# A cosformer attention and token-mixing kernel: at most six DMA transfers in flight instead of eight

## The chip, the cores and the metric

The kernel runs on one core of a Trainium2 chip. The metric is device time in microseconds (us), the median of a few runs. The engines are named as in the profile: PE is TensorE's matmul, PEld its weight load, DVE is VectorE, ACT is ScalarE, POOL is GpSimd, SP is SyncE. SP computes nothing in this kernel; its queue issues all 138 DMA transfers.

## What is computed

The inputs q, k and v have the shape (8, 8, 576, 64): batch, heads, sequence, head width, in fp32. Linear attention with cosine and sine weights comes first, and a token mixer over its output second:

```python
theta = np.pi / 2.0 * pos / S
phi(x) = concatenate([relu(x) * cos(theta), relu(x) * sin(theta)], axis=-1)
kv  = einsum('bhsf,bhsd->bhfd', phi(k), v);  z = sum(phi(k), axis=2)
x   = einsum('bhsf,bhfd->bhsd', phi(q), kv) / (einsum('bhsf,bhf->bhs', phi(q), z) + 1e-06)
# heads joined: x is (8, 576, 512)
W   = (x @ w_q) @ (x @ w_k).T / sqrt(64)          # per batch, 576 x 576
out = relu(W @ x) @ w_out                         # (8, 576, 512), fp32
```

## The kernel before

**Tiling.** The eight heads of a batch are taken as four head pairs, and two head pairs make one work unit H, of which there are 16 (two for each batch). A unit needs 128 x 2 x 576 fp32 elements of each of q, k and v. These arrive as two halves, a and b, each a transfer of 128 x 576 fp32, 288 KB. For each input there are five raw buffers (NRAW, line 101), so unit H shares its buffer with units H-5 and H+5.

**Work of a unit.** RK and RQ (lines 222 to 227) take the ReLU of k and q into bf16. V reaches bf16, multiplied by the cosine and sine table, in one of two ways: by a cast CV (line 229) and a product VS on DVE (line 232), or by the one step VG on POOL (line 239, its instruction at line 248). PE then makes kv (KV, line 268), transposes q (QT, line 290) and multiplies the two (N, line 332, instructions at line 340). The evacuations and the division follow on DVE and ACT. When both units of a batch are there, the mixer runs: WK, WQ, KX, MX (lines 434 to 492), and for each pair of batches nine output tiles WO (line 504, matmuls at line 509), their copy OE to one of 18 output buffers (line 512), and their store ST of 256 KB (line 518).

**Weights.** LW (line 521) loads w_q and w_k (128 KB each) and w_out in four transfers of 256 KB.

**What sets the order.** The string ORDER (lines 26 to 67) is a list of words, each one step. The loop at line 555 calls them in this order, and every engine gets its instructions in the order of the calls. So the 138 transfers stand in SP's queue in the order of the words LQ, LK, LV, LW and ST. SP is strictly in order: an instruction that waits holds all transfers behind it. Nothing in the order is decided at run time; engines wait for each other by semaphores.

**What a transfer waits for before the change.** The framework gives the transfers eight semaphores in turn, named DMAHW0 to DMAHW7 in the listings. A transfer may be issued when the one that had its semaphore before it, eight transfers earlier, has landed; so no more than eight are ever in flight. Besides, a load waits until the readers of its raw buffer are through with it, and a store until its output buffer has been written.

Of the kernel before, what the change touches and what calls it, by code (L numbers as in the profile page):

```python
# [70 lines left out]
def kernel(  # L71
# [10 lines left out]
    nc = tc.nc  # L82
# [4 lines left out]
    P = 128  # L87
# [12 lines left out]

    NRAW, NPREP, NV2, NQM, NX, NXT, NOUT = (5, 2, 2, 2, 2, 2, 18)
    XC = DM // 2
    EPS_PE = (9, 17, 20, 21)
    NUM_JOINT = ()
    WARM_COLS = 384
# [8 lines left out]
    def bufs(n, shape, dtype, name):  # L114
        return [pool.tile(shape, dtype, name=f"{name}{i}") for i in range(n)]

    raw = {nm: bufs(NRAW, [P, 2, HC], FP32, f"{nm}raw") for nm in "kqv"}
# [10 lines left out]
    wq_b = bufs(2, [P, HS], BF16, "wq")  # L128
    kx_b = bufs(2, [P, 2, XC], BF16, "kx")
    mix_b = bufs(2, [P, NDM, 2 * S], BF16, "mix")  # L130
    o_b = bufs(NOUT, [P, DM], FP32, "o")

    PS = psum.tile([P, 8, 2048], U8, name="ps")
    place = {}

    def srcs(src):
        return [src[b].flatten().rearrange("(pr p e) -> p pr e", pr=NPAIR, p=P)
                for b in range(B)]

    src = {"k": srcs(k), "q": srcs(q), "v": srcs(v)}  # L140

    def load(nm, H, part):
        b, h = divmod(H, 2)
        for r in (0, 1) if part is None else (part,):
            nc.sync.dma_start(raw[nm][H % NRAW][:, r, :], src[nm][b][:, 2 * h + r, :])  # L145

    coef = math.pi / 2.0 / S
    ki = pool.tile([P, C, 2], I32, name="ki")
# [5 lines left out]
    wq_f = pool.tile([P, NDM, DH], FP32, name="wqf")  # L154
    wk_f = pool.tile([P, NDM, DH], FP32, name="wkf")
    wo_f = pool.tile([P, NDM, DM], FP32, name="wof")
# [50 lines left out]
    def cast(eng, dst, s):  # L207
        if eng is A:
            A.copy(dst, s)  # L209
        elif eng is G:  # L210
            G.tensor_scalar(dst, s, 1.0, 1.0, op0=ALU.mult, op1=ALU.mult)  # L211
        else:
            V.tensor_copy(dst, s)  # L213
# [111 lines left out]
    def num(t):  # L325
        return pair(t).bitcast(FP32)[:, :, 0:SC * (D + 1)].rearrange("p w (u e) -> p w u e", u=SC)
# [5 lines left out]
    def N(g, ps, eng):  # L332
# [3 lines left out]
        for u in range(SC):  # L336
            for s in range(2):
                for pr in range(2):
# [4 lines left out]
                        start=(u == 0 and s == 0),  # L343
                        stop=(u == SC - 1 and s == 1 and g not in EPS_PE))
        if g in EPS_PE:
            for pr in range(2):
# [4 lines left out]
    def rec(g):  # L351
        return rec_b[g // 2 % 4][:, g % 2]
# [24 lines left out]
    def RC(g, ps, eng):  # L377
        V.reciprocal(rec(g), num(place["N", g])[:, :, :, D:D + 1] if g in EPS_PE else rec(g))

# [51 lines left out]
    def bank(i):  # L431
        return PS[:, i, :].bitcast(FP32)
# [28 lines left out]
    def KX(b, ps, eng):  # L461
        place["KX", b] = ps
        o = bank(ps)
        for u in range(SC):
            for t in range(2):
                nc.tensor.matmul(  # L466
                    o[H2 * t:H2 * t + H2, 0:XC], wk_b[b % 2][:, u, :],
                    x_b[b % NX][:, u].rearrange("p h d -> p (h d)")[:, t * XC:(t + 1) * XC],
                    start=(u == 0), stop=(u == SC - 1))

    def XK(b, ps, eng):
        cast(eng, kx_b[b % 2][:, 0, :], bank(place["KX", b])[:, 0:XC])

# [42 lines left out]
    out_t = out.flatten().rearrange("(t p e) -> t p e", t=NT, p=P)  # L516

    def ST(i, ps, eng):
        nc.sync.dma_start(out_t[i], o_b[place["OE", i]])

    def LW(i, ps, eng):
        if i == 0:
            nc.sync.dma_start(wq_f, moe_w_q.rearrange("(c p) j -> p c j", p=P))
        elif i == 1:
            nc.sync.dma_start(wk_f, moe_w_k.rearrange("(c p) j -> p c j", p=P))
        else:
            nc.sync.dma_start(wo_f[:, i - 2, :], moe_w_out[(i - 2) * P:(i - 1) * P, :])

    def CW(i, ps, eng):
        if i < 2:  # L530
# [13 lines left out]
    def WU(i, ps, eng):  # L544
        n, shape = divmod(i, 4)
        rows, cols = ((H2, H2), (H2, P), (P, P), (P, H2))[shape]
        for _ in range(n):
            nc.tensor.matmul(bank(ps)[0:cols, 0:WARM_COLS], wc[0:rows, WARM_COLS:WARM_COLS + cols],
                             wc[0:rows, 0:WARM_COLS], start=True, stop=True)

    steps = {f.__name__: f for f in (EJ, XJ, RC, RJ, TB, WU, KV, QT, KE, QM, N, EP, X, XT, XR, XE, WK, KW, WQ, QW, KX, XK, XA, XB,
                                     MX, ME, WO, OE, ST, LW, CW, TK, TV, TI, TQ, TW, T2, TZ)}
    halves = {f.__name__: f for f in (RK, RQ, CV, VS, VG)}

    for word in ORDER.split():
        word, _, eng = word.partition("@")
        word, _, ps = word.partition(":")
        part = {"a": 0, "b": 1}.get(word[-1])
        word = word.rstrip("ab")
        kind = word[:2] if word[:2] in steps or word[:2] in halves or word[0] in "LT" else word[0]  # L560
        i, ps = int(word[len(kind):] or 0), int(ps or 0)
        if kind in ("LK", "LQ", "LV"):
            load(kind[1].lower(), i, part)
        elif kind in halves:
            halves[kind](i, ps, ENG.get(eng), slice(0, 2) if part is None else
                         slice(part, part + 1))
        else:
            steps[kind](i, ps, ENG.get(eng))
# [30 lines left out]
```

## Time and profile before

| what | value |
|---|---|
| median of 3 runs | 117.97 us (117.83 to 118.92) |
| the profiled execution: its own time | 116.73 us |
| the profiled execution: span of the instructions | 114.9 us |
| what lies around the span | 1.8 us |
| PE busy, share of the span | 96.4 us, 84% |
| DVE, ACT, POOL busy | 87.0, 84.2, 73.1 us |
| bytes by DMA, mean rate | 39.38 MB, 343 GB/s |
| granted TensorE clock | 1.000 |

The page names, for each group of instructions, the line of the kernel, the engine, out<-in by the program's tile names, how often it ran, its busy time and what its engine waited for. For a DMA, the SP row gives the time at which the transfer was issued and how long SP was held by issuing it; the data move later. "To landing" is the time from the start of the issue until the last byte is signalled. The chain that ended last is followed back from the last instruction, at each step to what released it.

### The profile page before, as it was taken

Reading aid. Unit: us, or ns where it says so; the run is one execution under the profiler, and the core shown is the slowest. Engines: PE = TensorE matmul, PEld = TensorE weight load, DVE = VectorE, ACT = ScalarE, POOL = GpSimd, SP = SyncE. Lnnn points to the kernel's source line nnn. Section 1 sums busy time; section 2 is a strip of 40 time slices with the busy share of each in tenths; the row PEclk is TensorE's granted clock in tenths of the full one; section 3 lists DMA queues with packets and bytes.
Section 4 is the critical chain, followed back from the end, with each engine's and each line's share of the span. In section 5 each row is a group of like instructions: output and inputs, shape, how many; then the busy total and the mean of one; then the engine's idle time right before and its main releaser. Section 6 shows DMA issues by size and latency. Waiting matters only on the chain.

```text
span 114.9 us, 4999 instructions
## 1 busy us (share of the span) xinstructions
PE 96.4 (84%) x2126; PEld 64.7 (56%) x2126; DVE 87.0 (76%) x160; ACT 84.2 (73%) x153; POOL 73.1 (64%) x62
## 2 busy tenths in 40 slices
PE   0034776797898999999899999999999999999970
PEld 0034644685776877656685656646774676563420
DVE  2029999699899999799579967699897896750650
ACT  7543518788999986999699959879788849568520
POOL 7434059965779799937899996799999821010000
PEclk9999999999999999999999999999999999999999
DMA  3999999999999999999999999989889679886494
GB/s 87 318 376 401 401 379 340 385 391 391 389 390 390 387 388 388 386 385 380 389 382 398 393 397 387 376 288 325 271 281 324 242 267 366 339 336 260 185 374 174
DMA packets 20662, 39.38 MB, mean 343 GB/s; under 512 B 3232, under 2 KB 3232, under 8 KB 20640
## 3 DMA queue, kind: packets, MB, share of 16 engines
q1 hardware_dynamic: 20640, 39.07, 93.4%
q8 instruction: 16, 0.26, 1.0%
q14 instruction: 6, 0.05, 0.1%
HBM read 29.62 MB, written 9.44 MB: 340 GB/s over the span
## 4 chain that ended last, share of the span: by engine, by line
PE 57%; DMA 32%; POOL 5%; SPq 2%; ACT 1%; issue 1%; POOLq 0%
PE ps L509 29%; DMA vraw<-in_v_dram 21%; DMA wkf<-in_moe_w_k_dram 6%; PE ps L340 5%; DMA qraw<-in_q_dram 5%; PE ps L285 5%; POOL v L248 4%; PE ps L489 4%; PE ps L466 3%; PE ps L419 3%; PE ps L439 3%; PE ps L452 3%; SPq L145 2%; PE ps L301 1%; PE ps L295 1%
## 5 line engine op out<-in xcount | busy, mean ns | idle before, releaser
L248 POOL TENSOR_TENSOR v<-vraw,vtab 128x1152 bf16<-128x1152 f32 (+1 forms) x16 | 49.4, 3098 | 9.3 <-DMA vraw<-in_v_dram 8.3
L509 PE MATMUL ps<-wow,mix 128*128 128x512 bf16 x144 | 34.9, 381 | 0.0
L393 DVE TENSOR_TENSOR x<-ps,rec 128x640 bf16<-128x640 f32 x32 | 25.3, 820 | 0.7
L509 PEld LDWEIGHTS <-mix 128*128 128x128 bf16 x144 | 12.4, 98 | 14.1 <-issue 1.6
L209 ACT COPY o<-ps 128x512 f32<-128x512 f32 x25 | 14.6, 587 | 5.9 <-PE ps L509 5.4
L500 ACT ACTIVATE mix<-ps 128x576 bf16<-128x576 f32 x27 | 16.9, 651 | 2.0 <-PE ps L489 1.8
L203 ACT ACTIVATE rk<-kraw 128x576 bf16<-128x576 f32 (+1 forms) x18 | 14.6, 817 | 2.2 <-DMA kraw<-in_k_dram 1.8
L316 DVE TENSOR_TENSOR qm<-ps,qtab 128x1152 bf16<-128x1152 bf16 x22 | 15.4, 747 | 0.3 <-PE ps L295 0.3
L340 PEld LDWEIGHTS <-qm 64*128 64x128 bf16 x640 | 12.5, 96 | 4.4 <-issue 3.0
L340 PE MATMUL ps<-kvs,qm 64*128 64x65 bf16 x640 | 14.2, 193 | 0.9 <-ACT kvs L209 0.8
L203 ACT ACTIVATE rq<-qraw 128x576 bf16<-128x576 f32 (+1 forms) x15 | 11.6, 784 | 4.5 <-DMA qraw<-in_q_dram 4.5
L295 PE MATMUL ps<-ident,rq 128*128 128x128 bf16 x99 | 8.2, 234 | 7.9 <-POOL rq L205 7.7
L285 PE MATMUL ps<-v,rk 64*64 64x130 bf16 x432 | 9.3, 227 | 3.5 <-DVE v L234 1.3
L213 DVE COPY o<-ps 128x512 f32<-128x512 f32 x11 | 7.6, 689 | 6.2 <-PE ps L489 3.7
L295 PEld LDWEIGHTS <-rq 128*128 128x128 bf16 x99 | 6.4, 105 | 9.5 <-POOL rq L205 7.9
L205 POOL TENSOR_SCALAR rq<-qraw 128x576 bf16<-128x576 f32 (+1 forms) x10 | 8.6, 868 | 4.3 <-DMA qraw<-in_q_dram 3.7
L285 PEld LDWEIGHTS <-rk 64*64 64x64 bf16 x432 | 7.4, 111 | 6.8 <-ACT rk L203 2.0
L209 ACT CAST kvs<-ps 128x260 bf16<-128x260 f32 (+1 forms) x14 | 6.2, 442 | 4.0 <-PE ps L285 3.3
L211 POOL TENSOR_SCALAR kx<-kx 64x256 bf16<-64x256 bf16 x5 | 2.0, 399 | 10.4 <-ACT kx L209 10.1
L209 ACT COPY xT<-ps 128x1280 bf16<-128x1280 bf16 (+1 forms) x7 | 8.2, 1176 | 0.1
L234 DVE TENSOR_TENSOR v<-vb,vtab 128x1152 bf16<-128x1152 bf16 (+1 forms) x9 | 8.2, 926 | 0.1
L213 DVE COPY xT<-ps 128x1280 bf16<-128x1280 bf16 (+1 forms) x9 | 7.2, 805 | 1.4 <-PE ps L406 0.8
(66 smaller groups left out, 131.9 us busy)
## 6 DMA issues: line engine op xcount, KB each, us to landing
qraw<-in_q_dram SPq DMA_DIRECT2D x32, 288.0 KB, 5.9
vraw<-in_v_dram SPq DMA_DIRECT2D x32, 288.0 KB, 5.9
kraw<-in_k_dram SPq DMA_DIRECT2D x32, 288.0 KB, 5.9
out_dram<-o SPq DMA_DIRECT2D x36, 256.0 KB, 3.7
wof<-in_moe_w_out_dram SPq DMA_DIRECT2D x4, 256.0 KB, 5.7
wqf<-in_moe_w_q_dram SPq DMA_DIRECT2D x1, 128.0 KB, 6.7
wkf<-in_moe_w_k_dram SPq DMA_DIRECT2D x1, 128.0 KB, 6.6
```

The lines of the kernel that those rows point to most:

```text
L203: A.activation(dst, s, AF.Relu)
L205: eng.tensor_scalar(dst, s, FMAX, 0.0, op0=ALU.min, op1=ALU.max)
L209: A.copy(dst, s)
L213: V.tensor_copy(dst, s)
L248: G.tensor_mul(dst[:, part, :, :, 0:D], s[:, part].unsqueeze(3).to_broadcast([P, n, C, 2, D]), vtab.unsqueeze(1).to_broadcast([P, n, C, 2, ...
L285: nc.tensor.matmul(kv_v[o, r, :], rk_of(H)[a, pr, c, :], v2_b[H % NV2][a, pr, c, :, 0:D + 1], start=(c == 0), stop=(c == C - 1))
L295: nc.tensor.transpose(qt_v[:, c, :], rq_b[H % NPREP][:, c, :, :], ident)
L316: V.tensor_mul(qm_b[H % NQM][:, :, r, 0:C, :], q_t[:, r].unsqueeze(1).to_broadcast([P, 2, C, H2]), qtab)
L340: nc.tensor.matmul(nv[:, pr, u, :], qm_b[H % NQM][a, s, r, 2 * u:2 * u + 2, :], kv_b[H % 2][a, r, pr if H in KV_WIDE else 0, s, 0:D + 1], ...
L393: V.tensor_tensor(x_b[b % NX][:, :, 4 * h:4 * h + 4, :].rearrange("p u (w r) d -> p r w u d", r=2)[:, r], nv[:, :, :, 0:D], rec(g).to_broa ...
L500: A.activation(dst, s, AF.Relu, scale=scale_moe)
L509: nc.tensor.matmul(o, mix_b[bp % 2][:, m, rt * P:(rt + 1) * P], wow[:, m, :], start=(m == 0), stop=(m == NDM - 1))
```

## The change

A helper `dma` issues every transfer and keeps a list of what it has issued. From the seventh transfer on, it adds a dependency on the transfer that was issued six earlier. The words, their order, the buffers and all other steps stay as they are.

```diff
+    IN_FLIGHT = 6
...
+    in_flight = []
+
+    def dma(dst, s):
+        i = nc.sync.dma_start(dst, s)
+        if len(in_flight) >= IN_FLIGHT:
+            tc.add_manual_dep(
+                i.ins, in_flight[-IN_FLIGHT].ins.name,
+                mybir.DependencyInfo(mybir.DependencyClass.Sync, mybir.DependencyReason.DATA),
+                reason="transfers in flight")
+        in_flight.append(i)
...
-            nc.sync.dma_start(raw[nm][H % NRAW][:, r, :], src[nm][b][:, 2 * h + r, :])
+            dma(raw[nm][H % NRAW][:, r, :], src[nm][b][:, 2 * h + r, :])
...
-        nc.sync.dma_start(out_t[i], o_b[place["OE", i]])
+        dma(out_t[i], o_b[place["OE", i]])
...
-            nc.sync.dma_start(wq_f, moe_w_q.rearrange("(c p) j -> p c j", p=P))
+            dma(wq_f, moe_w_q.rearrange("(c p) j -> p c j", p=P))
...
-            nc.sync.dma_start(wk_f, moe_w_k.rearrange("(c p) j -> p c j", p=P))
+            dma(wk_f, moe_w_k.rearrange("(c p) j -> p c j", p=P))
...
-            nc.sync.dma_start(wo_f[:, i - 2, :], moe_w_out[(i - 2) * P:(i - 1) * P, :])
+            dma(wo_f[:, i - 2, :], moe_w_out[(i - 2) * P:(i - 1) * P, :])
```

On SP this moves waits, as three places of its queue show. In these rows qraw, kraw and vraw are raw buffers (the number behind the name tells which of the five), o is an output buffer, and a wait on Activation, DVE or Pool is one for a buffer's reader or writer. All transfers of the changed kernel stand at line 146, the helper's, where before they stood at the lines of load, ST and LW.

The first place is the start of the queue. Before:

```order
L145 DMA kraw_64<-in_k_dram 128x576 x2
L145 DMA vraw_73<-in_v_dram 128x576 x2
L145 DMA qraw_68<-in_q_dram 128x576 [waits DMAHW0_49]
L145 DMA qraw_68<-in_q_dram 128x576 [waits DMAHW1_49]
L145 DMA kraw_63<-in_k_dram 128x576 [waits DMAHW2_49]
```

And with the change:

```order
L146 DMA kraw_64<-in_k_dram 128x576 x2
L146 DMA vraw_73<-in_v_dram 128x576 [waits DMAHW0_49]
L146 DMA vraw_73<-in_v_dram 128x576 [waits DMAHW1_49]
L146 DMA qraw_68<-in_q_dram 128x576 [waits DMAHW2_49]
L146 DMA qraw_68<-in_q_dram 128x576 [waits DMAHW3_49]
L146 DMA kraw_63<-in_k_dram 128x576 [waits DMAHW4_49]
```

The first wait for a landing stood at the ninth transfer, for the first one (DMAHW0); it stands now at the seventh, and the ninth waits for the third.

The second place is around the 47th transfer, LV6b, one of the two halves of v that the POOL step VG of unit 6 needs. Before:

```order
L145 DMA qraw_69<-in_q_dram 128x576 [waits DMAHW5_49]
L145 DMA vraw_74<-in_v_dram 128x576 [waits DMAHW6_49]
L145 DMA kraw_64<-in_k_dram 128x576 [waits DMAHW7_49]
L145 DMA vraw_74<-in_v_dram 128x576 [waits DMAHW0_49]
L527 DMA wof<-in_moe_w_out_dram 128x512 [waits DMAHW1_49]
```

And with the change:

```order
L146 DMA qraw_69<-in_q_dram 128x576 [waits DMAHW7_49]
L146 DMA vraw_74<-in_v_dram 128x576 [waits DMAHW0_49]
L146 DMA kraw_64<-in_k_dram 128x576 [waits DMAHW1_49]
L146 DMA vraw_74<-in_v_dram 128x576 [waits DMAHW2_49]
L146 DMA wof<-in_moe_w_out_dram 128x512 [waits DMAHW3_49]
```

The rows are the same transfers in the same order; each names the semaphore two further on, which belongs to the transfer six earlier. No second wait was added, since a landing six back takes the place of one eight back.

The third place is among the late stores. Before:

```order
L519 DMA out_dram<-o_122 128x512 [waits DMAHW1_49,DVE_49]
L519 DMA out_dram<-o_118 128x512 [waits DMAHW2_49]
L519 DMA out_dram<-o_117 128x512 [waits DMAHW3_49]
L519 DMA out_dram<-o_114 128x512 [waits DMAHW4_49]
L519 DMA out_dram<-o_121 128x512 [waits DMAHW5_49,Activation_49]
```

And with the change:

```order
L146 DMA out_dram<-o_122 128x512 [waits DMAHW3_49,DVE_49]
L146 DMA out_dram<-o_118 128x512 [waits DMAHW4_49]
L146 DMA out_dram<-o_117 128x512 [waits DMAHW5_49]
L146 DMA out_dram<-o_114 128x512 [waits DMAHW6_49]
L146 DMA out_dram<-o_121 128x512 [waits DMAHW7_49,Activation_49]
```

The stores' waits for DVE and ACT stand where they stood.

## The prediction

> **What bounds the kernel now.** The first view is the page: its account of the DMA, slice by slice, and the chain that ended last.
>
> ```profile
> DMA  3999999999999999999999999989889679886494
> GB/s 87 318 376 401 401 379 340 385 391 391 389 390 390 387 388 388 386 385 380 389 382 398 393 397 387 376 288 325 271 281 324 242 267 366 339 336 260 185 374 174
> PE 57%; DMA 32%; POOL 5%; SPq 2%; ACT 1%; issue 1%; POOLq 0%
> ```
>
> The transfers run at 376 to 401 GB/s in nearly every slice up to slice 26 (about 75 us) and fall off behind it. The chain is 32% DMA and 57% PE. The chain in order of time tells where each has its part:
>
> ```profile
> 3.53 5.81 DMA vraw<-in_v_dram
> 9.34 0.02 issue
> 9.36 6.00 DMA vraw<-in_v_dram
> ...
> 15.38 6.56 DMA wkf<-in_moe_w_k_dram
> ...
> 22.00 5.94 DMA qraw<-in_q_dram
> ...
> 28.01 6.12 DMA vraw<-in_v_dram
> 34.13 0.02 issue
> 34.15 5.95 DMA vraw<-in_v_dram
> 40.09 0.02 issue
> ...
> 40.26 4.73 POOL v L248 x2
> 44.98 0.04 issue
> 45.02 0.72 PE ps L285 x36
> ```
>
> Until 40.09 us the chain is nothing but transfers. Each starts 0.02 us after another has landed: the eight semaphores are a window, and when one transfer lands the one eight places on is issued. Then comes one POOL step for unit 6, and from 45 us PE alone. So two stages have two limits, and the windows put numbers to them (the last three columns are the clock, the DMA share and GB/s):
>
> ```profile
> 10.00:45.00 35.00, 29.62 (x718) 23.67 (x718) 32.74 (x64) 27.10 (x46) 26.06 (x18) 1.00 1.06 386
> 45.00:75.00 30.00, 29.41 (x710) 19.39 (x711) 24.27 (x42) 25.72 (x49) 24.81 (x18) 1.00 1.04 386
> 75.00:105.00 30.00, 30.00 (x662) 18.12 (x661) 23.64 (x42) 22.51 (x44) 17.65 (x9) 1.00 0.86 305
> ```
>
> From 10 to 45 us the DMA engines are full (share 1.06) and PE has gaps (29.62 of 35). From 45 us PE has hardly any (29.41 of 30, then 30.00 of 30). What the change does to the landings of the first 40 us reaches the end about one for one; what it does later must first make PE run dry.
>
> **The change, part by part.** It removes no transfer, adds no instruction and moves none. Each wait of SP for a landing moves from eight places back to six. Behind it on SP stand all later transfers, and all loaders of raw data wait for those. So the question is one inequality: is the DMA still full with six?
>
> The spacing of the transfers, and the time of one from issue to landing, stand in SP's timeline and in the rows for the load line in three stretches: the very first transfer (0 to 1 us), the full stretch from 16 to 41 us, and 76 to 86 us, where the queue is half empty.
>
> ```profile
> 9.36 0.33 SPq L145 DMA_DIRECT2D vraw<-in_v_dram  x1
> ...
> 13.87 0.34 SPq L145 DMA_DIRECT2D vraw<-in_v_dram  x1
> ```
>
> ```profile
> DMA to landing us min/median/max: 2.9/2.9/2.9
> ```
>
> ```profile
> DMA to landing us min/median/max: 5.5/5.9/6.6
> ```
>
> ```profile
> DMA to landing us min/median/max: 3.9/4.3/5.6
> ```
>
> Between 9.36 and 13.87 us lie six spacings (three input transfers in between are merged in one row or left out here): 4.51 / 6 = 0.75 us a transfer. In the full stretch a transfer takes 5.9 us, and 8 x 0.75 is 6.0: it spends most of that time queued behind the seven ahead of it. Alone it took 2.9 us, 0.75 of which is its own moving, so about 2.15 us are the way there and back.
>
> With six in flight a full queue gives 6 x 0.75 = 4.5 us from issue to landing. The queue stays full if a transfer needs less than that when nothing is ahead of it, with the 0.02 us that SP takes to wake: 2.9 + 0.02 = 2.92. The margin is 4.5 - 2.92 = 1.58 us; now it is 6.0 - 2.92 = 3.08. **Cost of the smaller window while nothing disturbs it: 0.** What hides it is the queue of transfers already handed over. Without that cover, at an unqueued time of 4.5 us or more, each tenth above would cost 0.1 / 6 = 0.017 us a transfer.
>
> The 2.9 us were measured on an idle memory, and under load it could be more. The bound from the other side is the half-empty stretch, 4.3 us in the median, where some of it is still queueing (the DMA share from 75 us on is still 0.86). Even 4.3 fits, with a margin of 0.18. I take 2.9, because in that stretch a transfer also waits for those ahead of it, which the full stretch already counts in its 0.75.
>
> **The start.** The seventh transfer was issued at 3.53 us, the eighth behind it, the ninth at 4.55 (timeline of SP, and the time to landing of that ninth alone):
>
> ```profile
> 3.53 0.98 SPq L145 DMA_DIRECT2D vraw<-in_v_dram  x2
> 4.55 1.54 SPq L145 DMA_DIRECT2D qraw<-in_q_dram  x2
> 6.37 1.16 SPq L145 DMA_DIRECT2D kraw<-in_k_dram  x2
> ```
>
> ```profile
> DMA to landing us min/median/max: 6.3/6.3/6.3
> ```
>
> Now the seventh waits for the first, issued at 0.74 us and landed 2.9 later, at 3.64: 0.1 us of delay. The ninth waits for the third. In the old kernel the third's landing released the eleventh (the 6.37 row), so the ninth goes out near 6.4, 1.8 us later than before. It used to land at about 4.55 + 6.3 = 10.8 and needs 6.4 + 2.9 = 9.3 at the least. Cost 0, cover 1.5 us.
>
> **Holds of SP.** Some issues hold SP for longer than 0.33 us. In the stage that counts, these are of that kind:
>
> ```profile
> 16.88 0.93 SPq L145 DMA_DIRECT2D qraw<-in_q_dram  x1
> 24.21 0.83 SPq L145 DMA_DIRECT2D qraw<-in_q_dram  x1
> 30.23 1.02 SPq L145 DMA_DIRECT2D kraw<-in_k_dram  x1
> 36.40 0.62 SPq L527 DMA_DIRECT2D wof<-in_moe_w_out_dram  x1
> ```
>
> The excess over 0.33 is 0.60, 0.50, 0.69 and 0.29 us, 2.08 together. Each comes alone, six us from the next, and is below the margin of 1.58, so each is made good before the next: cost 0. If the margin were gone, the 2.08 us would be the price. A fetch of instructions uses the same engines:
>
> ```profile
> q8 instruction: 16, 0.26, 1.0%
> ```
>
> Sixteen fetches share 1.0% of 16 engines' 114.9 us, 1.15 us each on average, again below 1.58, and one comes every 7 us on average.
>
> **Behind 75 us** SP no longer waits for landings, but for the engines that fill the output buffers (waits of SP from 75 us):
>
> ```profile
> SPq L519 <- DVE o L213: 4.4, 4, 2.4
> SPq L519 <- ACT o L209: 4.0, 6, 1.2
> SPq L519 <- DVE rec L359: 3.4, 1, 3.4
> SPq L519 <- ACT kvs L209: 2.0, 1, 2.0
> ```
>
> Where the wait for six is the later one, as in a burst of stores, the store was queued anyway and lands when it did, so whoever waits for an output buffer is not later. That wait is small (the view of waits), and the last eight stores meet no cap (the store line from 106 us):
>
> ```profile
> ACT o L209 <- DMA out_dram<-o: 0.2, 1, 0.2
> ```
>
> ```profile
> L519 SPq DMA_DIRECT2D out_dram<-o x8: 332/332/383, 106.9 to 111.9; - x8
> ...
> DMA to landing us min/median/max: 2.0/2.1/2.3
> ```
>
> Eight issues in 5.0 us are 0.71 apart; at 2.1 us each, three are in flight. **Cost 0**, and the end stays at the last store.
>
> The sum: 0 + 0 + 0 + 0. Span 114.9 and 1.8 around it give 116.7, as the profiled execution had; it lies 1.2 below the median of the three runs, 117.97, and the forecast is for the median: **118.0 us**.
>
> One rule of the Trainium skill speaks against this. "DMA: Bandwidth & Descriptors", section "Anatomy of one DMA — SWDGE (gpsimd) path", gives a transfer on another queue than this one about 2.0 us fixed plus its bytes at 436 GB/s. Read as a price of each window, by estimate eight of 288 KB would take 7.4 us and six 6.1, 0.93 and 1.01 us a transfer, hence 0.08 more for each of some 40 transfers, 121.3 us in all. The trace disagrees with that reading at eight: 0.75, not 0.93. Its mechanism is rival B below.
>
> **The rivals.**
>
> *A: the margin is not there (slower).* Place: the load queue from 5 to 45 us. If the unqueued time under load is near the 4.3 us of the half-empty stretch, 0.18 us is left and each hold of SP shows: 2.08 - 4 x 0.18 = 1.36 us on the four quoted, 119.3 us. It decides from the point where margin and hold meet: at the longest excess, 0.69, that is an unqueued time of 4.5 - 0.02 - 0.69 = 3.8 us. For it: the half-empty stretch does show 3.9 to 5.6. Against: those include queueing, and the first transfer took 2.9.
>
> *B: a window costs a fixed round (slower).* If the 2.15 us were paid once a window, eight would be 2.15 + 8 x 0.48 = 6.0, six 2.15 + 6 x 0.48 = 5.04, which is 0.84 a transfer and 0.09 more. From the eighth to the 47th transfer, the one that lands at 40.09 us, 39 x 0.09 = 3.5 us: 121.5. Against it: issues come evenly 0.75 us apart and the DMA share is 1.06, with no gap in a round.
>
> *C: less queueing helps (faster).* A share of 1.06 says that packets overlap in an engine. If fewer queued transfers let instruction fetches through sooner, the chain's "issue" part could shrink. That is 1% of the span, 1.1 us at the utmost: 116.8 us. For it: fetches do share the engines. Against: an engine has work queued all the time at six as at eight, so a fetch meets the same neighbour.
>
> *D: the cap does not bind.* Where eight semaphores already rule, a cap could be empty. SP's order shows it is not: the seventh transfer now waits for the first. If it did nothing, the time would be 118.0, told apart only by the time to landing.
>
> **How the numbers follow.** Forecast 0.74, A 0.14, B 0.05, C 0.05, D 0.02. The three runs of before differ by 0.9%, so about 1% can be told from no change, 116.8 to 119.2. A at 119.3 lies just outside: 0.10 slower, 0.04 within. B is slower, 0.05. C is at the bound: 0.03 faster, 0.02 within. Of the forecast's 0.74 I give 0.03 to each side for the scatter of such runs; D is within. That makes 0.06 faster, 0.76 within, 0.18 slower. The range takes in the forecast with its scatter, C's end and A: 116.9 to 119.7 us; B is left out.
>
> **What would show it.** Right: loads in the full stretch land 4.4 to 4.6 us after issue instead of 5.9, still 0.75 us apart; 10 to 45 us stays within 380 to 392 GB/s; the POOL step of unit 6 starts at 40.3 us within 0.4; PE stays at 29 to 30 of 30 us from 45 us. A would show as landings late by some tenths behind each long issue and that POOL step 1 to 1.5 us late; B as 340 to 350 GB/s from 10 to 45 us; C as the same landings with a shorter PE stage. The forecast is wrong if the rate from 10 to 45 us drops by over 2%, or if PE waits for loads behind 45 us.

## The result and the profile after

The changed kernel takes 126.6 us (median of 6 runs, 124.5 to 130.6), the kernel before 117.9 us (median of 6, 117.2 to 119.8). The ratio is 1.065, 95% interval 1.059 to 1.071: slower by 6.5%, and outside the range that was given. The ratio is taken from the quicker runs of each kernel alone, and the profiled execution is not one of them (130.1 us, span 128.3), so its rows show more of the loss than the ratio has.

The page of the changed kernel, the rates by slice and the shares of the chain:

```profile
GB/s 122 311 404 351 366 374 279 292 389 341 356 301 362 335 340 320 372 333 327 384 362 283 327 286 337 294 356 254 283 178 272 304 286 234 389 122 359 131 377 183
DMA 58%; PE 23%; ACT 6%; POOL 4%; SPq 3%; issue 2%; DVE 1%; POOLq 0%; ACTq 0%
```

Where the old kernel ran at 376 to 401 GB/s in nearly every slice, this one jumps between 279 and 404 from slice to slice up to 86 us. The DMA's share of the chain rose from 32 to 58%: PE no longer sets the pace from 45 us on. The same three stretches as before:

```profile
10.00:45.00 35.00, 29.17 (x646) 23.26 (x645) 30.95 (x56) 24.68 (x43) 23.16 (x17) 0.95 1.00 340
45.00:75.00 30.00, 25.90 (x602) 16.74 (x601) 22.03 (x42) 22.13 (x41) 23.73 (x17) 1.00 0.98 334
75.00:105.00 30.00, 25.20 (x638) 15.71 (x634) 21.86 (x37) 20.44 (x40) 19.80 (x10) 1.00 0.84 286
```

The rate fell from 386 to 340 and 334 GB/s, and PE, full before from 45 us, has gaps of 4 to 5 us in each later stretch. The granted clock is 0.95 in the first stretch and 1.00 in the second, where the rate is no better, so the clock is not what slows the transfers. The POOL step of unit 6, which began at 40.26 us, begins at 43.55, since the load that it needs lands at 43.39 us instead of 40.09:

```profile
43.55 4.71 POOL L260 TENSOR_TENSOR v<-vraw,vtab 128x1152 bf16<-128x1152 f32 x2 [1.44 <-PE ps L287]
```

How the loss comes about is seen on SP. First the longest waits for a landing up to 45 us; the columns are the total, the number and the longest. Before:

```profile
SPq L145 <- DMA qraw<-in_q_dram: 5.4, 14, 0.4
SPq L145 <- DMA kraw<-in_k_dram: 4.3, 11, 0.7
```

After:

```profile
SPq L146 <- DMA qraw<-in_q_dram: 8.3, 13, 1.8
SPq L146 <- DMA kraw<-in_k_dram: 7.0, 15, 1.1
```

The number of waits is nearly the same; some of them are now up to 1.8 us long. The timeline of SP shows the first of these:

```profile
14.69 0.38 SPq L146 DMA_DIRECT2D wqf<-in_moe_w_q_dram  x1
15.42 1.08 SPq L146 DMA_DIRECT2D vraw<-in_v_dram  x2
18.36 0.38 SPq L146 DMA_DIRECT2D wkf<-in_moe_w_k_dram  x1
19.03 0.33 SPq L146 DMA_DIRECT2D kraw<-in_k_dram  x1
```

From 16.50 to 18.36 us SP hands nothing over, because one landing is late; in the rows shown the issues before and after this gap are about 0.7 us apart. In all transfers from the 10th to the 91st, the median distance between two landings is 0.73 us (0.75 in the old kernel): between the gaps the DMA is as quick as ever. Sixteen landings came more than 0.9 us after the one ahead of them (four before), and what they have above 0.75 adds up to 12.3 us (2.3 before). That is 10 us more, and the 91st transfer landed 9.1 us later (82.4 us instead of 73.3), so these late landings account for what the loads lost up to there. The semaphore records show who is late. A transfer's landing is signalled by 16 DMA engines, each for its part. The seventeenth transfer was done on 15 engines between 15.74 and 16.88 us, and on the last at 18.34. The trace has an instruction packet of 16 KB at 16.30 us. In the old kernel the same thing happens, with a packet at 16.34 us: the landing at 18.55 us came 1.68 us after the one ahead of it, its last engine 0.93 us behind the other 15. These had gone on with what was already handed over, and were through with the next transfer by 18.48 us.

### The profile page after: what moved, and what is told of

It reads as the page before. It is cut to its first block, busy times and chain, and to the rows that moved or that the text cites. A ratio compares the mean times of both kernels' runs of the same rounds, so it can differ in the third digit from the quotient of the medians.

```text
span 128.3 us, 4999 instructions
## 1 busy us (share of the span) xinstructions
PE 99.6 (78%) x2126; PEld 66.4 (52%) x2126; DVE 87.4 (68%) x160; ACT 84.1 (66%) x153; POOL 73.5 (57%) x62
## 4 chain that ended last, share of the span: by engine, by line
DMA 58%; PE 23%; ACT 6%; POOL 4%; SPq 3%; issue 2%; DVE 1%; POOLq 0%; ACTq 0%
DMA kraw<-in_k_dram 21%; DMA qraw<-in_q_dram 16%; PE ps L521 12%; DMA vraw<-in_v_dram 9%; DMA wof<-in_moe_w_out_dram 8%; DMA out_dram<-o 4%; SPq L146 3%; ACT rq L215 2%; PE ps L297 2%; POOL v L260 2%; PE ps L501 2%; PE ps L352 2%; PE ps L431 1%; PE ps L464 1%; PE ps L451 1%
## 5 line engine op out<-in xcount | busy, mean ns | idle before, releaser
L307 PE MATMUL ps<-ident,rq 128*128 128x128 bf16 x99 | 8.8, 244 | 10.9 <-POOL rq L217 7.7
L297 PE MATMUL ps<-v,rk 64*64 64x130 bf16 x432 | 10.0, 242 | 7.1 <-ACT rk L215 1.8
L297 PEld LDWEIGHTS <-rk 64*64 64x64 bf16 x432 | 8.1, 120 | 10.5 <-ACT rk L215 2.9
L307 PEld LDWEIGHTS <-rq 128*128 128x128 bf16 x99 | 6.9, 109 | 12.7 <-POOL rq L217 8.1
L332 DVE TENSOR_TENSOR qm<-ps,qtab 128x2304 bf16<-128x2304 bf16 x5 | 6.8, 1354 | 4.2 <-PE ps L313 4.2
L501 PE MATMUL ps<-wq,kx 64*128 64x288 bf16 x64 | 8.0, 287 | 0.6 <-POOL kx L223 0.6
(66 smaller groups left out, 128.3 us busy)
```

The source lines that it names most:

```text
L297: nc.tensor.matmul(kv_v[o, r, :], rk_of(H)[a, pr, c, :], v2_b[H % NV2][a, pr, c, :, 0:D + 1], start=(c == 0), stop=(c == C - 1))
L307: nc.tensor.transpose(qt_v[:, c, :], rq_b[H % NPREP][:, c, :, :], ident)
L501: nc.tensor.matmul(pair(ps)[:, t, :].bitcast(FP32)[:, 0:HS], kx_b[b % 2][a, (m // 2) ^ t, (m % 2) * P:(m % 2 + 1) * P], wq_b[b % 2][a, :], ...
```

## The experiments

Two kinds of kernels follow. The first kind is the whole kernel with another window. The second leaves the computation out and keeps the transfers, so that its time is theirs. All ratios are to the kernel before on the same chip.

**Seven in flight.**

```diff
-    IN_FLIGHT = 6
+    IN_FLIGHT = 7
```

> Seven transfers in flight instead of six. Theory R (run-ahead): a transfer is spread over 16 DMA engines and lands when the slowest of them is done; an instruction fetch holds one engine at a time for over 1 us, and the window sets how far the other 15 may run ahead meanwhile. Each place more in the window buys 0.75 us of run-ahead, so seven keeps a part of the loss: 119 to 122 us, between 117.9 with eight and 124.5 to 126.6 with six. Theory L (loop time): six is less than one transfer's way there and back, about 4.9 us under load, and costs at every transfer alike; seven gives 7 x 0.75 = 5.25 us, which is enough: 117.5 to 118.5 us.

Measured: 118.8 us, ratio 1.013 (1.006 to 1.020). One place more buys back four fifths of the loss. That is below the range of R, which had 119 us as its lower end, and above L's; the windows have 382 GB/s from 10 to 45 us and 368 from 45 to 75. It told little between the two.

**Six for the first 48 transfers only, and six from the 49th only.**

```diff
-        if len(in_flight) >= IN_FLIGHT:
+        if IN_FLIGHT <= len(in_flight) < 48:     # the first 48 only
...
+        if len(in_flight) >= 48:                 # from the 49th only
```

> The cap of six holds for the first 48 transfers alone (up to the load that the POOL step of unit 6 needs); behind that the framework's eight. R and L: the loads up to there land about 3.3 us late, as in the changed kernel, and PE, full from then on, gives nothing back: 120.5 to 121.5 us. Rival P (placing): the loss arises only once stores mix in and output buffers come free late; then this kernel runs at 117.5 to 118.5 us.

> The cap of six holds from the 49th transfer on alone. R: the stage from 45 us is PE's as long as loads come in time, but each fetch costs up to 1 us of landing and no loss is made good, so loads fall behind PE: 120 to 123 us. If PE's stage has slack for it, as the prediction had it (PE full, DMA behind it): 117.5 to 118.5 us. P: 124 us or more.

Measured: 120.8 us, ratio 1.022 (1.007 to 1.036), and 122.0 us, 1.037 (1.027 to 1.048). Each is within R's range (the first within L's too). The windows of the first and of the second:

```profile
10.00:45.00 35.00, 27.89 (x639) 22.51 (x639) 30.62 (x56) 24.43 (x43) 22.33 (x17) 0.95 0.98 333
45.00:75.00 30.00, 28.20 (x663) 18.95 (x663) 24.38 (x46) 24.61 (x45) 26.00 (x19) 1.00 1.05 394
```

```profile
10.00:45.00 35.00, 29.66 (x717) 23.69 (x713) 32.24 (x63) 26.86 (x46) 25.92 (x18) 1.00 1.04 375
45.00:75.00 30.00, 25.94 (x574) 16.72 (x569) 21.89 (x38) 21.69 (x41) 22.32 (x17) 0.96 0.98 331
```

The rate falls where the cap holds, 333 and 331 GB/s, and nowhere else; with eight places again it is 394 at once. (The 375 of the second kernel is 385 up to 38 us and 337 from there to 45: its cap starts with the 49th transfer, issued at 36.9 us.) 2.2 and 3.7% add up to 5.9 of the 6.5%. So rival P (the placing among the stores) falls, and PE's stage has no slack for late loads: with the cap there alone PE is busy for 25.94 of 30 us, where it had 29.41.

**Six in flight, adjacent halves merged; and the same with eight.**

```diff
+        if part is None:
+            dma(raw[nm][H % NRAW], src[nm][b][:, 2 * h:2 * h + 2, :])
+            return
...
+    for n, w in enumerate(words[1:]):
+        if w[0] == "L" and w[:-1] == words[n][:-1] and {w[-1], words[n][-1]} == {"a", "b"}:
+            words[n], words[n + 1] = w[:-1], ""
```

> Six transfers in flight still, but where the two halves of one input stand next to each other in the order, they go out as one transfer of 576 KB (125 - 1 transfers instead of 138; the same bytes in the same order of units). R: what counts is the bytes that each DMA engine has ahead of it, and those grow by about a fifth on the average: 118 to 122 us, clearly below the 124.5 to 126.6 of the changed kernel. Rival N (number): each landing costs a wake-up of SP and that is what six in flight exposes; the loss shrinks only with the number of transfers, a tenth: 123.5 us or more.

> Adjacent halves in one transfer of 576 KB, and the framework's eight in flight: the control of the run with six in flight and merged halves (126.3 us), and a try at a kernel better than before. If bytes ahead of an engine are all that counts: 115.5 to 117.9 us, below the kernel before. If merging has a price of its own, because the first half is usable only when both are there: 118.5 us or more, and the price has to be taken off the other run.

Measured: six 126.3 us (123.3 to 128.3; no interval), eight 118.6 us, 1.014 (1.007 to 1.022). Merging has a small price of its own, and six with merging lose about as much against eight with merging as six lose without, as far as four runs that lie 5 us apart can tell. R as I had put it missed, and 126.3 us is within N's range. I had called the gain in bytes a fifth, but only 15 of 123 transfers are merged, an eighth. A stretch where merged transfers stand close together has a higher rate; from 30 to 38 us the merged kernel, and then the changed one:

```profile
30.00:38.00 8.00, 6.24 (x145) 5.10 (x146) 6.44 (x10) 6.37 (x11) 6.05 (x7) 1.00 1.03 391
```

```profile
30.00:38.00 8.00, 6.53 (x148) 5.41 (x150) 7.36 (x14) 6.92 (x13) 6.04 (x7) 1.00 0.98 332
```

The kernel with the cap on the first 48 transfers has 347 GB/s in this stretch. This is one profile of each, so a hint and no more. The total left the matter open, so it was tried again below with transfers alone.

**Transfers alone, eight and six in flight, few and many PE instructions.**

```diff
-    for word in ORDER.split():
-        ...
+    for n in range(440):      # few; many: range(1700), and 64 columns
+        nc.tensor.matmul(bank(n % 8)[:, 0:512], wc[:, WARM_COLS:WARM_COLS + P], wc,
+                         start=True, stop=True)
+    for word in ORDER.split():
+        # only loads and stores; output buffers zeroed once
...
```

> Leaves out the computation: all 138 transfers in the same order with the same buffers, the output buffers filled with zeros once, eight in flight; PE runs 440 matmuls of 128x512 on constants beside them, about 880 instructions, so few instruction fetches. Its time is the transfers' own: about 138 x 0.75 = 103 us, 100 to 108 us in all theories; it is the base for the next three.

> As the one before (computation left out, 440 long matmuls on constants), with six in flight. R: few fetches, so few engines are held: within 0.5 to 3 us of the kernel with eight. L: six are not enough for the loop, fetches or not: slower by 6 us or more (4.9 / 6 = 0.82 us a transfer instead of 0.75 gives 138 x 0.07 = 9 us).

> Computation left out, eight in flight, but PE runs 1700 matmuls of 128x64 on constants, about 3400 instructions in about the same time, so some 13 instruction fetches instead of 3 or 4. R: eight in flight absorb most of them: 0 to 4 us above the kernel with few. L: no difference but for the bytes of the fetches, below 1 us.

> Computation left out, six in flight, 1700 short matmuls. R: some ten fetches more than with the long matmuls, each 0.5 to 1 us of landing: 5 to 10 us above six in flight with few fetches, and as much above eight in flight with many. L: the same time as six in flight with few.

| in flight | 440 long matmuls, 3 instruction packets of 16 KB | 1700 short ones, 13 packets |
|---|---|---|
| 8 | 106.4 us (ratio 0.909, 0.903 to 0.915) | 108.6 us (0.929, 0.924 to 0.934) |
| 6 | 111.9 us (0.949, 0.941 to 0.957) | 116.5 us (113.3 to 118.1) |

Both theories were half wrong. Ten more packets cost 2.2 us with eight in flight. With six they cost 4.6 by the medians, but 2.5 between the quickest runs (110.8 and 113.3 us), so that they cost more with the short window, as R has it, is likely and not shown. Six lose 5.6 us with three packets already, which R had put at 0.5 to 3 and L at 6 or more. Thirteen landings (of the 10th to the 91st) are more than 0.9 us behind the one ahead in that kernel, and the median distance is 0.73 us, so it is again isolated late landings and not L's slower pace throughout. Two of the thirteen, at 13.6 and 21.3 us, came before the first packet, at 22.9.

**Two, four and seven in flight, transfers alone.** Edit: the number of IN_FLIGHT.

> Computation left out, two in flight. Nearly idle DMA engines; spacing x 2 is the unqueued time. With the 2.9 us of the first load and 2.0 of a late store: (102 x 2.9 + 36 x 2.0) / 2 = 184 us and a little for the start: 180 to 195 us under R'. If the first load was unusually quick and 3.6 us (the shortest with six in flight) is the rule: 215 us or more.

> Computation left out, 440 long matmuls, four in flight. It measures the loop: spacing x 4 is the time from issue to landing under load when almost nothing queues. R' (the loop is short, what six in flight exposes are single late engines): between 2.9 and 3.4 us, so 0.75 to 0.85 us a transfer and 110 to 125 us in all. L (the loop itself is about 4.6 us under load): 1.15 us a transfer, 155 us or more.

> Computation left out, seven in flight. R': between eight (106.4) and six (111.9): 106.8 to 109 us, the single late engines being covered in part. L: a loop of 4.6 to 5.0 us is below 7 x 0.75 = 5.25, so as with eight: 106.0 to 106.8 us.

Measured: 197.5, 133.8 and 106.7 us (ratios 1.686, 1.142 and 0.910). Two in flight came out just above the range of R', four between the two ranges, and seven in L's. Time from issue to landing of the loads issued from 20 to 60 us, with two, with four and with six:

```profile
DMA to landing us min/median/max: 2.3/3.0/4.1
```

```profile
DMA to landing us min/median/max: 2.9/4.1/5.0
```

```profile
DMA to landing us min/median/max: 4.1/4.9/6.2
```

Four in flight at the quick 2.9 us would be 0.73 us a transfer, a full DMA; it ran at 283 GB/s from 10 to 50 us. So 2.9 us is the usual time while at most one other transfer is in flight (3.0 in the median with two), and the quickest with four. Half of those take over 4.1, some 5; part of this is queueing behind the three others, and the runs do not tell how much. Six places cover 4.5 us, within that spread; seven cover 5.25, its edge, and eight 6.0.

**Whole inputs of 576 KB, four and three in flight, transfers alone.**

```diff
-        for r in (0, 1) if part is None else (part,):
-            dma(raw[nm][H % NRAW][:, r, :], src[nm][b][:, 2 * h + r, :])
+        dma(raw[nm][H % NRAW], src[nm][b][:, 2 * h:2 * h + 2, :])
```

> Computation left out, 440 long matmuls; each input of a unit is one transfer of 576 KB (1.5 us of moving), four in flight. Theory T (tail): what counts is the work that an engine still has when a landing lets the next transfer out, (in flight - 1) x the time of one, against the late part of the time on the way. Four whole ones leave 3 x 1.5 = 4.5 us, as seven halves do (6 x 0.75): 385 GB/s or more from 10 to 50 us, 107 us plus up to 1.5 for the stores, of which four leave only 1.9 us. Theory N (number): four in flight are four, 284 GB/s as with four halves.

> As before with three whole transfers in flight. T: 2 x 1.5 = 3.0 us are left, less than the 3.75 of six halves and more than the 2.25 of four: between 284 and 356 GB/s from 10 to 50 us, about 320. If bytes in flight alone counted (3 x 576 KB are 6 x 288 KB): 356 GB/s as with six halves. N: below 284 GB/s.

Measured: 111.7 us, 0.948 (0.934 to 0.962), and 129.4 us (126.6 to 129.6). The windows of the four whole ones and of the three:

```profile
10.00:50.00 40.00, 39.79 (x183) 18.12 (x185) 1.01 (x3) 0.00 (x0) 1.00 1.02 369
```

```profile
10.00:50.00 40.00, 39.79 (x183) 18.19 (x186) 1.01 (x3) 0.00 (x0) 1.00 0.92 304
```

Put in order of the work that is left when a landing lets the next transfer out (in flight less one, times 0.75 or 1.5 us), the rates from 10 to 50 us are: 0.75 us 185 GB/s (two halves), 2.25 us 283 (four), 3.0 us 304 (three whole), 3.75 us 362 (six), 4.5 us 383 (seven) and 369 (four whole), 5.25 us 386 (eight). Neither the number nor the bytes in flight alone give such an order: four whole ones are far above four halves, and three whole ones far below six halves. T's figures were 385 and 320, so it is right in order and a twentieth too high; its time for four whole ones, 108.5 us at most, was passed by 3 us. N's 284 GB/s for four falls.

**Six in flight, and what makes the engines late.** Edits to the kernel with 440 matmuls: 8 matmuls; 220 matmuls; 110 matmuls in fp32 (the fp32 kernel), which keep PE as busy with a quarter of them.

> Computation left out, six halves in flight, and PE runs 8 matmuls instead of 440, so no instruction fetch falls into the run. If the late engines are made by fetches: 106 to 108 us, as with eight in flight. If a DMA engine is late without them too, once it runs dry under load: 110 to 112.5 us, as with 440 matmuls.

> Computation left out, six halves in flight, and PE runs 220 long matmuls instead of 440, so it works in the first half of the run alone. If late engines need PE's work or its fetches beside them: from 10 to 45 us about 362 GB/s as with 440 matmuls, behind 50 us about 398 as with 8. If the disorder, once there, stays: about 352 GB/s behind 50 us too.

> Computation left out, six halves in flight, PE busy all the time with 110 fp32 matmuls of 128x512, each longer than a bf16 one, so that hardly an instruction fetch falls into the run. If fetches make the engines late: 106 to 107.5 us, as with 8 matmuls. If it is PE's work as such (its reading of the memory that the transfers write): 110 to 112.5 us, as with 440 matmuls in bf16.

Measured: 106.5 us, 0.907 (0.891 to 0.923); 110.3 us, 0.938 (0.926 to 0.951); 111.2 us, 0.945 (0.930 to 0.961). With PE silent and no 16 KB instruction packet, six in flight are as quick as eight. The windows of that kernel:

```profile
10.00:50.00 40.00, 0.00 (x0) 0.00 (x0) 1.01 (x3) 0.00 (x0) 0.50 1.04 377
50.00:90.00 40.00, 0.00 (x0) 0.00 (x0) 0.00 (x0) 0.00 (x0) 0.50 1.05 398
```

The time of the fp32 kernel lies in the range that stood for PE's work as such (110 to 112.5 us) and not in the one for the packets. Its profile tells otherwise. It has one 16 KB instruction packet in its run, at 48.3 us, and PE is busy on both sides of it. Its page, then its windows, then SP around that time:

```profile
GB/s 79 294 389 385 375 400 350 358 393 390 390 393 392 392 388 391 391 391 370 319 317 379 313 351 359 355 401 336 342 342 368 388 402 405 408 407 408 404 267 0
...
q8 instruction: 1, 0.02, 0.1%
```

```profile
10.00:48.00 38.00, 36.15 (x78) 15.87 (x79) 1.60 (x4) 0.00 (x0) 1.00 1.05 384
50.00:88.00 38.00, 38.00 (x90) 16.85 (x89) 0.00 (x0) 0.00 (x0) 1.00 1.00 353
```

```profile
46.17 2.59 SPq L146 DMA_DIRECT2D kraw<-in_k_dram  x4
50.64 1.10 SPq L146 DMA_DIRECT2D vraw<-in_v_dram  x2
```

Up to the packet, six in flight run at 384 GB/s beside a busy PE: the loop is not too long, and PE's work does not slow the transfers. Then SP stands still from 48.76 to 50.64 us, since the landing at 50.62 us has its last engine 1.44 us behind the other 15. The rate is 353 GB/s for the next 38 us, without another such packet: eight more landings are over 0.9 us behind the one ahead. The semaphore records show that the engines have come apart: from the first engine to the last, a transfer's landing took 0.7 us in the median from 30 to 48 us, and 1.7 from 50 to 88. The kernel with 220 matmuls, whose PE stops at half time, bears this out in part:

```profile
50.00:90.00 40.00, 1.09 (x6) 0.29 (x3) 0.00 (x0) 0.00 (x0) 0.54 1.02 372
```

With PE silent in this stretch, it has 372 GB/s, not the 398 of the kernel whose PE was silent throughout, but more than the 352 that were forecast for a disorder that stays. It starts at 388 GB/s (50 to 60 us) and has 359 from 80 to 90, so PE need not work for landings to come late. So a delay of one engine can leave the 16 engines out of step for long, and with six in flight further differences between them show as late landings. Eight in flight come apart too, but do not lose by it: in the kernel with 440 matmuls the landing at 25.4 us has one engine 1.58 us late, the landings then stay spread over 2.5 us in the median up to 88 us, and the rate is 386 GB/s from 10 to 50 us and 397 from 50 to 90. Nor does every delay last with six: in the kernel with 8 matmuls a landing at 15.6 us came 1.26 us after the one ahead, its last engine 0.52 behind, without any packet, and the rate rose from 349 GB/s (10 to 16 us) to 392 (30 to 50 us).

That the packet starts the disorder in the fp32 kernel rests on its time in this one profile and on the undisturbed 38 us ahead of it. That late landings come without one is seen in the kernels with 8 and with 440 matmuls. What makes single engines late without a packet, and which delays are made good, stays open.

No version beat the kernel before: seven in flight, merging with eight and both partial caps are slower by 1.3 to 3.7%.

## Why the prediction was wrong

- **What bounds the kernel**: half right. Loads set the pace to 45 us, and the cap on the first 48 transfers alone reached the end (2.2%). Behind 45 us the prediction left PE in charge, but the DMA ran at 386 GB/s there too, and the cap from the 49th transfer on alone cost 3.7%.
- **The change on SP**: right. Only the waits moved, and their number stayed.
- **The inequality**: it held for as much as it claims. "Cost of the smaller window while nothing disturbs it: 0" is borne out by 377 GB/s and 106.5 us with PE silent, and by 384 GB/s in the fp32 kernel up to its packet. The margin of 1.58 us behind it was too large a reserve: 2.9 us is the quickest transfer with four in flight, where the median is 4.1 and the slowest 5.0, over the 4.5 that six places cover. The other bound, 4.3 us, was set aside, though it left 0.18.
- **Holds and fetches**: the step that failed. "Each comes alone, six us from the next, and is below the margin of 1.58, so each is made good before the next: cost 0." It treated the DMA as one queue, in which a delay eats into a reserve that refills. A landing is the last of 16 engines, and one late engine closes the window for all: SP stood still for 1.86 us at 16.50 us in the changed kernel. The delay was not made good either: after one packet of about 1 us the fp32 kernel ran at 353 GB/s instead of 384 for 38 us. In the changed kernel such late landings make up 12.3 us to the 91st transfer, against 2.3 before. The price of one of them stood in the quoted row of before at 16.88 us, whose next issue came 1.68 us later instead of 0.75. I read the hold of SP in it and not the late landing.
- **The start**: right. The ninth transfer went out at 5.99 us and took 4.9, so it landed at 10.9 us, as before.
- **Behind 75 us, cost 0**: wrong in the profiled execution. The chain that ended last was PE's there, and now passes through a load of v that was issued at 96.82 us and landed at 104.01. ACT had waited 0.2 us in the whole run for a store to land, and now waits three times, once behind 75 us, for 2.1 us:

```profile
ACT o L221 <- DMA out_dram<-o: 4.6, 3, 2.1
```

- **Rival A** had the direction and half of the place: it left out the loads behind 45 us. Its condition, an unqueued time over 3.8 us, is not shown (3.0 us in the median with two in flight). Its price of 1.36 us counted SP's holds and left the late landings out; the medians differ by 8.7 us.
- **Rival B** named the rate that was found (340 GB/s from 10 to 45 us), by a mechanism that is not there: six run at 384 GB/s until something disturbs them. A number that fits does not prove the cause.
- **A price paid by every window**: the Trainium skill, "DMA: Bandwidth & Descriptors", section "Anatomy of one DMA — SWDGE (gpsimd) path", states a fixed time and a time for the bytes of each DMA; read as the price of a window, this gave 121.3 us by estimate. The runs at six in flight disagree with that reading: 377 and 384 GB/s in undisturbed stretches. That the time went up, as it had it, was luck. **C** and **D** fell: no stage became shorter, and the cap binds.

## What to carry to other kernels

Here a window of transfers had to cover the slow end of the time on the way under load, not the quickest transfer, with a reserve for a delay of one DMA engine: 4.5 us (six) lost 6.5%, 5.25 us (seven) 1.3%. A quick check is the transfers alone at half the window: spacing times window gives the time on the way under load, some queueing included. When the median spacing of landings is unchanged and the rate is lower, look for isolated late landings, and then at which of the engines' parts came last.

## What was not expected of the hardware

- A 16 KB instruction packet can go with one DMA engine of 16 being late. Behind the four packets from 16.3 to 36.4 us of the changed kernel a landing came 1.4 to 2.2 us after the one ahead instead of 0.75, its last engine 0.65 to 1.46 us behind the others. With eight in flight the packets at 23.6 and 35.5 us left no such gap. The number of packets goes with PE's instructions: none with 8 matmuls, 3 with 440, 13 with 1700, 16 in the full kernel.
- The disorder can outlast its cause: 353 GB/s for 38 us after one packet with six in flight. With eight places the rate was 394 GB/s directly after the cap ended.
- PE at full work does not slow the transfers as such (384 GB/s beside 36.15 of 38 us busy).
